# Four sequences through mLSTM, Fourier mix and MLP: a second folded batch, named PSUM banks, and two recurrences started later

## The chip, the cores and the metric

The kernel runs on one core of a Trainium2 chip. The core has a matrix engine (TensorE, "PE" in the profile; its weight loads are listed apart as "PEld"), a vector engine (VectorE, "DVE"), a scalar engine (ScalarE, "ACT"), a general engine (GpSimd, "POOL") and a queue engine (SyncE, "SP") that issues most DMA transfers. Each engine works through its own queue in program order and waits on semaphores for the others. PE writes its results to PSUM, eight banks in this kernel; DVE and ACT read them from there. The metric is the device time of one launch in microseconds (us): the median of several runs. Everything is float32.

## The reference, cut to what matters

Four batches, 8 heads, 768 steps, 40 numbers per head. A gated recurrence gives `y`, the heads are joined to 320 columns, and a Fourier mix followed by a two-layer MLP is applied, with residuals:

```python
for t in range(S):
    m_new = np.maximum(f_gate[:, :, t] + m, i_gate[:, :, t])
    f_stab = np.exp(f_gate[:, :, t] + m - m_new)
    i_stab = np.exp(i_gate[:, :, t] - m_new)
    C = f_stab * C + i_stab * np.einsum('bhd,bhe->bhde', vt, kt)
    n = f_stab * n + i_stab * kt
    y[:, :, t] = sigmoid(o_gate_t) * (C @ qt) / np.maximum(np.abs(n @ qt), 1.0)

X = np.fft.fft(np.fft.fft(x, axis=1), axis=2)        # x: (4, 768, 320)
u = x + np.real(X)
un = (u - mean(u)) / np.sqrt(var(u) + 1e-06)
out = u + np.maximum(un @ w_ch1, 0.0) @ w_ch2        # 320 -> 1280 -> 320
```

(The recurrence is abbreviated: broadcasts are left out.)

## The kernel before

The batches are numbered b = 0 to 3 in the code; "second batch" is b = 1. Each goes through three stages, and different batches are in different stages at the same time.

**Recurrence.** The 768 tokens of a batch are six chunks c = 0 to 5 of 128. A chunk is computed in matrix form on PE: scores of queries with keys, products with the values, and a state that is carried from chunk to chunk (all these small products stand on L547). For b = 1, 2, 3 `plan_halves` spaces the chunks three slots apart. Of a chunk planned at slot s: loads on SP at s − 6 (q and k, L484; k and v, L486), gate tables and masks soon after, the output gate at s − 2; `mlstm_scale_q` (POOL, L528) at s − 2; `mlstm_scale_v` (POOL) and `mlstm_exp` (ACT) at s − 1; scores and state products on PE at s; `halves_decay` (POOL) and `halves_add` (DVE, L703, "C add") at s, s + 1 and s + 2; `halves_weigh` (DVE, L708) at s + 1; `halves_from_state` and `halves_from_chunk` (PE) at s + 3; `mlstm_finish` (DVE, L752 to L759) at s + 4, which reads the heads' PSUM banks and writes the chunk's 128 tokens into x. All chunks share those heads' banks, so `halves_from_state` of a chunk waits for `mlstm_finish` of the chunk before.

**Fourier mix.** The real part of the two-dimensional transform is two sets of products with cosine and sine tables. Tokens t and 768 − t are first folded into sums and differences (`mix_fold`, on DVE, and POOL for small parts), pair p = 2, 1, 0 as their chunks are finished; x_done are the slots of that. For b = 2 and 3 they are folded once more (`mix_fold_again`, L860 the first of its two DVE operations), so that each product covers only every other table column: `mix_products_again` (L903) instead of `mix_products` (L912, L913, L915). `mix_seq` and `mix_tail` issue those products into PSUM tiles pz (two) and pzt, which are copied to SBUF as Z and Zt. `mix_feat` multiplies them with the feature tables into a tile pu for each p (L946). `mix_add` (DVE, L963 to L974) adds pu to the tokens of two chunks, one call for each, and takes the statistics; `mix_center` (ACT, L982) subtracts the mean; `mix_turn` (PE, L989) transposes a token block into a tile put, and `mix_turn_out` (ACT, L994) copies it out.

**MLP.** The first layer in `mlp_in` for b = 0 (L1067, L1058) and in blocks of four steps for b > 0 (L1129, L1134, with DVE's h adds on L1138); the second in `mlp_out` for b = 0 (L1192) and `mlp_out_pair` for b > 0 (L1248), into tiles po; the residual with the row's scale is DVE's L1198, and the store follows it on SP (L1201).

**Order.** A plan written by hand sets it: `at(slot, phase, function, ...)` puts a call into a slot and a phase, and the calls are issued in the order of (slot, phase). The phases are EVAC 0, FILL 1, MAIN 2 and FILL_PE 3, with fractions between. Each engine's queue has that order; a call in a later slot can therefore stand in the way of one that another engine waits for, on any of the five queues. The MLP of b = 0 lies in slots 31 to 62 (its `mlp_out` in 51 to 62), that of b = 1 in 63 to 94 (blocks to 82, pairs from 83), b = 2 in 95 to 126, b = 3 from 127. The mix of b = 1 starts at slot 54, of b = 2 at 83, of b = 3 at 115. The recurrences start at 32, 51 and 83.

**Banks.** Four PSUM banks hold all tiles of the mix and the MLP (pz, pzt, pu, put, pm, po). Each has a pool tag with one buffer, so a new tile in a bank waits until the last reader of the tile before it is done, also when this reader stands in a later slot. `bank(name, shape, n)` takes bank n, or, without n, the next one of a string written out by hand. `MIX` names banks: "z" for pz, "zt" for pzt, "u" for pu in the order p = 0, 1, 2, "ut" for put in the order of `ORDER` (0, 5, 1, 4, 2, 3).

Of the kernel before, what the change touches and what calls it, by code (L numbers as in the profile page):

```python
# [19 lines left out]
L = 128  # L20
# [6 lines left out]
DM = H * D  # L27
# [3 lines left out]
TG = NT // 2  # L31
# [5 lines left out]
NC = HALF_D + 1  # L37
COL = (0, L + 1, 2 * L + 2)
LAST = 2 * L + 1
NK = HALF + 2  # L40
# [7 lines left out]
ORDER = (0, 5, 1, 4, 2, 3)  # L48
# [9 lines left out]
def kernel(  # L58
# [34 lines left out]
    def bank(name, shape, n=None):  # L93

        return ps_m.tile(shape, FP, name=name, tag=f"pm{next(turn) if n is None else n}")
# [34 lines left out]
    def at(slot, phase, fn, *args):  # L130
        plan.setdefault((slot, phase), []).append((fn, args))
# [7 lines left out]
    EVAC, FILL, MAIN, FILL_PE = range(4)  # L139
# [406 lines left out]
    def product(out, w, x, start):  # L546
        nc.tensor.matmul(out, w, x, start=start, stop=True, skip_group_check=True)  # L547
# [234 lines left out]
    def plan_halves(b, s0, stride=3):  # L782
        at(s0 - 2, FILL + 0.7, halves_start, b)
        for c in range(NT):
            s = s0 + stride * c
            end = c == NT - 1
            t = 22 + 2 * c if b == 1 and c < 3 else s - 6
            at(t, FILL, mlstm_load, b, c)
            at(t, FILL, mlstm_load_max, b, c)
            at(t + 1 if c < 2 or b > 1 else s - 5, FILL, mlstm_load_decay, b, c)  # L790
            at(s - 2, FILL, mlstm_load_o, b, c)
            at(s - 2, FILL + 0.1, mlstm_scale_q, b, c)
            at(s - 2, FILL + 0.15, halves_alone, b, c)
            at(s - 1, FILL, mlstm_scale_v, b, c)
            at(s - 1, FILL, mlstm_exp, b, c, 0)
            at(s - 1, FILL + 0.5, mlstm_exp, b, c, NP)
            at(s, FILL, mlstm_mask, b, c)
            at(s, FILL_PE + 2.05, halves_scores, b, c)
            at(s, FILL_PE + 2.5, halves_to_state, b, c)
            for i in range(2):  # L800
                at(s + i, FILL + 0.05, halves_decay, b, c, i)
                at(s + 1 + i, FILL - 0.2, halves_add, b, c, i)
            at(s + 1, FILL, halves_weigh, b, c)
            at(s + 3, MAIN - 0.1 if end else FILL_PE, halves_from_state, b, c)
            at(s + 3, MAIN if end else FILL_PE + 0.5, halves_between, b, c)
            at(s + 3, FILL_PE + 3, halves_from_chunk, b, c)
            at(s + 3, FILL_PE + 0.6, mlstm_tanh, b, c)
            at(s + 4 + int((b, c) in ((2, 2), (3, 1))), FILL + 0.05, mlstm_finish, b, c)

# [4 lines left out]

    mixes = {}

    MIX = {"z": (2, 3), "zt": 2, "u": (3, 2, 2), "ut": (3, 3, 3, 3, 2, 3)}

    def copy(eng, out, in_):
        (nc.scalar.copy if eng == 0 else nc.vector.tensor_copy)(out=out, in_=in_)
# [41 lines left out]
    def mix_seq(b, p, parts):  # L864


        k = mixes.setdefault(b, Mix())
        if p == TG - 1:
            k.pz = getattr(k, "pz", []) + [bank("pz", [L, NK], MIX["z"][i] if b > 1 else None) for i in parts]
        for i in parts:  # L870
            if b < 2:
                mix_products(p, k.pz[i], i, slice(0, L))
            else:
                for product in mix_products_again(k, k.pz[i], i, slice(0, L)):
                    product()

    def mix_tail(b, p):

        k = mixes[b]
        if p == TG - 1:  # L880
            k.pzt = bank("pzt", [L, NK], MIX["zt"] if b > 1 else None)
        halves = [k.pzt[i * 64:(i + 1) * 64] for i in range(2)]
        if b < 2:
            for i in range(2):
                mix_products(p, halves[i], i, slice(L, PAD))
        else:

            a, z = (mix_products_again(k, halves[i], i, slice(L, PAD)) for i in range(2))
            for product in (a[0], z[0], a[1], z[1], a[2], z[2], a[3]):
                product()  # L890
# [17 lines left out]
    def mix_products(p, out, i, m):  # L908
        fm = slice(i * PAD + m.start, i * PAD + m.stop)
        kw = dict(stop=(p == 0), skip_group_check=True)  # L910
        if i == 0 and p == TG - 2:
            nc.tensor.matmul(out[:, 1:NK:2], fe[:, p, fm], ds_sb[:, p, 0, 1:NK:2], start=False, **kw)  # L912
            nc.tensor.matmul(out[:, 0:NK:2], fe_odd[:, m], ds_sb[:, p, 0, 0:NK:2], start=False, **kw)  # L913
        else:
            nc.tensor.matmul(out, fe[:, p, fm], ds_sb[:, p, i], start=(p == TG - 1), **kw)  # L915
# [12 lines left out]
    def mix_feat(b, p):  # L928

        k = mixes[b]
        m = slice(COL[p], COL[p] + L)
        pu = k.pu[p] = bank("pu", [L, DM + 1 + NC], MIX["u"][p] if b > 1 else None)
        if b == 0:
            products = ((pu[:, 0:DM + 1], k.Z[:, 0, m], dd_sb[:, 0]), (pu[:, 0:DM + 1], k.Z[:, 1, m], dd_sb[:, 1]),
                        (pu[:, 0:DM + 1], k.Zt[:, m], dd_sb[:, 2]))
        else:
            products = ((pu[:, 0:NC], k.Z[:, 0, m], dd_sb[:, 0, 0:NC]), (pu[:, NC:DM], k.Z[:, 1, m], dd_sb[:, 1, 1:HALF_D]),  # L940
                        (pu[:, 0:DM], k.Zt[:, m], dd_sb[:, 3, 0:DM]))
        if p == TG - 2:
            last, own = slice(LAST, LAST + 1), pu[0:1, DM + 1:]
            products += ((own, k.Z[:, 0, last], dd_sb[:, 0, 0:NC]), (own, k.Zt[:, last], dd_sb[:, 3, 0:NC]))
        for i, (o, z, t) in enumerate(products):
            nc.tensor.matmul(o, z, t, start=(i == 0), stop=(i in (2, 4)), skip_group_check=True)  # L946
# [37 lines left out]
    def mix_turn(b, c):  # L984

        k = mixes[b]
        pt = k.pt[c] = bank("put", [L, 3, L], MIX["ut"][ORDER.index(c)] if b > 1 else None)
        for ch in range(3):
            nc.tensor.transpose(pt[:, ch, :], k.uc[c].rearrange("p two n -> p (two n)")[:, ch * L:(ch + 1) * L], ident)  # L989

# [27 lines left out]
    def plan_mix(b, s0, x_done, s_feat, s_add, s_turn):  # L1018
        for j in range(TG):
            p = TG - 1 - j  # L1020
            at(x_done[j] + (b > 1 and j == TG - 1), FILL + 0.5 if b < 2 else FILL_PE + 0.2, mix_fold, b, p)
            if b == 0:
                at((s0 - 4, s0 - 2, s0)[j], FILL_PE + 4, mix_seq, b, p, (0, 1))
                at((s0 - 2, s0 - 2, s0)[j], FILL_PE + 4, mix_tail, b, p)
            elif b == 1 or j == 0:
                if b > 1:
                    for step, slot in enumerate((x_done[-1] + 2, x_done[-1] + 6)):
                        at(slot, FILL_PE + 0.25, mix_fold_again, b, step)
                at(s0, FILL_PE + 4, mix_seq, b, p, (0,))
                at(s0 + 1, FILL_PE + 4, mix_seq, b, p, (1,))  # L1030
                at(s0 + 2, FILL_PE + 4, mix_tail, b, p)
        for i in range(2):
            at(s0 + 1 if b == 0 else s0 + 1 + i, FILL, mix_seq_out, b, i)
        at(s0 + (1 if b == 0 else 3), FILL + 0.1, mix_tail_out, b)
        for p in range(TG):
            at(s_feat[p], FILL_PE + 4, mix_feat, b, p)
        for c, a, t in zip(ORDER, s_add, s_turn):
            at(a, FILL if b < 2 else MAIN + 0.5, mix_add, b, c)
            at(t, FILL + 0.1, mix_center, b, c)
            at(t, FILL_PE + (5 if b == 0 or c in ORDER[:4] else -0.1), mix_turn, b, c)  # L1040
            if b > 0:
                at(t, FILL_PE + 6, mix_turn_out, b, c)
            elif t < s_mlp:
                at(t + 1, FILL + 0.2, mix_turn_out, b, c)
            else:
                at(t + 1, EVAC, mix_turn_out, b, c)
# [31 lines left out]
    def hidden(gr, f):  # L1078
        return hid[gr, f % 2][:, f // 2 * TG * L:(f // 2 + 1) * TG * L]
# [107 lines left out]
    def mlp_out(b, gr, i, half):  # L1187
        k = mixes[b]
        if half == 0:
            k.po = bank("po", [L, DM])  # L1190
        for f in range(half * NFF // 2, (half + 1) * NFF // 2):
            nc.tensor.matmul(k.po, hidden(gr, f)[:, i * L:(i + 1) * L], w2_sb[:, f, :], start=(f == 0), stop=(f == NFF - 1))  # L1192

# [83 lines left out]
    MLP_SLOTS = NT // TG * (NFF + 2 * TG)  # L1277
# [69 lines left out]
    s_mlp = 31  # L1347
    plan_batch(0, 0, 22, s_mlp)
    plan_batch(1, 32, 54, s_mlp + MLP_SLOTS)
    plan_batch(2, 51, 83, s_mlp + 2 * MLP_SLOTS)  # L1350
    plan_batch(3, 83, 115, s_mlp + 3 * MLP_SLOTS)
    for n in range(4):
        at(s_mlp + 2 * NFF + 1 + n, FILL + 0.4, weight_sums, n)
        at((56, 57, 58, 75)[n], FILL + 0.4, out_weight_sums, n)
# [162 lines left out]
```

## Time and profile before

| | us |
|---|---|
| runs of the kernel | 402.89, 404.14, 404.44 (median 404.14) |
| the profiled execution | 404.67, its span 402.9 |
| PE busy | 387.8 |
| DVE busy | 279.8 |
| ACT busy | 178.5 |
| POOL busy | 128.0 |

The profile shows one execution. A line of a group or of the timeline gives start and duration, engine, line of the code, operation, output and inputs, and in square brackets how long the engine was idle ahead of it and what ended that. The line of PE's waits gives the total, how often, and the longest. Over the span the mean granted clock of PE is 0.991. The DMA engines are most busy in the first 110 us; the mean over the span is 109 GB/s.

### The profile page before, as it was taken

To read this page: it belongs to the slowest core of one execution; us is meant where nothing else is said; L and a number is where in the kernel's file an instruction comes from. 1 tells how busy PE (TensorE), PEld (TensorE's weight loads), DVE (VectorE), ACT (ScalarE), POOL (GpSimd) and SP (SyncE) were. 2 spreads that over 40 slices of the span, in tenths; PEclk is the share of its full clock that TensorE was granted. 3 is DMA by queue.
4 is the path that set the end of the run, shared out by engine and by line. 5 is a ranking of instruction groups with operands and counts; after the bars stand their busy time and mean duration, and the time that the engine had idled before them with its cause. 6 is when DMAs were issued, how large, how long until landed. Compare 5 with 4: busy or idle time off the path is not lost.

```text
span 402.9 us, 10837 instructions
## 1 busy us (share of the span) xinstructions
PE 387.8 (96%) x4324; PEld 283.3 (70%) x4324; DVE 279.8 (69%) x668; ACT 178.5 (44%) x513; POOL 128.0 (32%) x231
## 2 busy tenths in 40 slices
PE   8999999999969999999999998999999999999996
PEld 6887555556546776856569887855579997556996
DVE  7789976898867519787665689777663795336652
ACT  6898867576530213553562214544440023454000
POOL 5744425466945412261145304351200000020000
PEclk9999999989989999999999999999999999999999
DMA  7979499677752424365100525300000000000000
GB/s 197 278 227 320 121 240 257 194 242 240 191 151 70 142 87 131 109 196 150 54 26 2 157 82 170 103 20 2 1 0 18 17 34 33 2 0 0 34 34 34
DMA packets 22766, 43.96 MB, mean 109 GB/s; under 512 B 3492, under 2 KB 11388, under 8 KB 22588
## 3 DMA queue, kind: packets, MB, share of 16 engines
q1 hardware_dynamic: 22716, 43.27, 36.0%
q8 instruction: 34, 0.56, 0.5%
q14 instruction: 16, 0.13, 0.1%
HBM read 39.16 MB, written 4.10 MB: 107 GB/s over the span
## 4 chain that ended last, share of the span: by engine, by line
PE 80%; DVE 13%; issue 2%; POOL 2%; ACT 2%; DMA 0%; DVEq 0%; SPq 0%; POOLq 0%; ACTq 0%
PE po L1248 20%; PE pm L1129 16%; PE po L1192 8%; PE pm L1134 6%; PE ph L547 5%; PE ps L547 4%; PE pu L946 4%; PE pm L1067 4%; PE put L989 2%; PE pz L903 1%; PE pz L915 1%; DVE so L756 1%; PE pM L230 1%; PE pm L1058 1%; DVE x L759 1%
## 5 line engine op out<-in xcount | busy, mean ns | idle before, releaser
L1138 DVE TENSOR_TENSOR h<-h,pm 128x384 f32<-128x384 f32 x60 | 30.7, 550 | 30.6 <-PE pm L1129 16.5
L1198 DVE SCALAR_TENSOR_TENSOR x<-po,rstd,x 128x160 f32<-128x160 f32 (+1 forms) x69 | 27.0, 394 | 35.0 <-PE po L1248 32.3
L1129 PE MATMUL pm<-uT,w_sb 128*128 128x384 f32 x90 | 37.8, 507 | 0.2 <-DVE uT L1117 0.2
L543 POOL TENSOR_SCALAR_AFFINE_SELECT W<-W 64x512 f32<-64x512 f32 x36 | 27.9, 775 | 31.5 <-ACT W L518 30.4
L696 POOL TENSOR_TENSOR C<-C,decB 128x164 f32<-128x164 f32 x33 | 17.4, 528 | 62.1 <-DVE C L703 58.4
L518 ACT ACTIVATE W<-W,colT 128x64 f32<-128x64 f32 x144 | 36.5, 338 | 0.0
L1192 PE MATMUL po<-w_sb,h 128*128 128x320 f32 x120 | 35.2, 444 | 0.0
L1013 POOL TENSOR_TENSOR t<-rstd 128x6 f32<-128x6 f32 x12 | 2.6, 216 | 90.1 <-DVE v L1007 89.7
L1248 PE MATMUL po<-T,S 128*128 128x160 f32 x180 | 28.1, 303 | 2.6 <-DVE x L1198 2.6
L528 POOL TENSOR_TENSOR qg<-qk,Gb 128x512 f32<-128x512 f32 x21 | 27.3, 1298 | 9.5 <-DMA Gb<-G_d 9.5
L1192 PEld LDWEIGHTS po<-w_sb,h 128*128 128x128 f32 x120 | 22.7, 194 | 10.0 <-issue 1.5
L1067 PE MATMUL pm<-uT,w_sb 128*128 128x384 f32 x80 | 29.5, 505 | 0.1
L1248 PEld LDWEIGHTS po<-T,S 128*128 128x128 f32 x180 | 25.3, 190 | 4.5 <-DVE x L1198 3.4
L1248 PE MATMUL po<-w_sb,h 128*128 128x160 f32 x180 | 26.3, 300 | 0.0
L1248 PEld LDWEIGHTS po<-w_sb,h 128*128 128x128 f32 x180 | 25.2, 190 | 1.5 <-DVE x L1198 0.3
L994 ACT COPY uT<-put 128x384 f32<-128x384 f32 x24 | 11.1, 478 | 32.7 <-PE put L989 32.6
L1134 PE MATMUL pm<-uT,w1t_sb 64*128 64x384 f32 x120 | 25.2, 510 | 0.2 <-DVE h L1138 0.2
L1129 PEld LDWEIGHTS pm<-uT,w_sb 128*128 128x128 f32 x90 | 15.4, 189 | 14.0 <-DVE h L1138 4.9
L1185 ACT ACTIVATE h<-h 128x384 f32<-128x384 f32 x45 | 23.1, 520 | 2.0 <-DVE h L1138 2.0
L982 ACT ACTIVATE uc<-x 128x384 f32<-128x384 f32 x24 | 14.5, 614 | 18.9 <-DVE x L974 18.9
L703 DVE TENSOR_TENSOR C<-C,ps 128x164 f32<-128x164 f32 x33 | 10.5, 317 | 16.2 <-PE ps L547 13.6
L1067 PEld LDWEIGHTS pm<-uT,w_sb 128*128 128x128 f32 x80 | 14.5, 194 | 9.7 <-issue 1.4
(240 smaller groups left out, 860.8 us busy)
## 6 DMA issues: line engine op xcount, KB each, us to landing
kvt<-in_kv SPq DMA_DIRECT2D x24, 336.0 KB
qk<-in_qkT SPq DMA_DIRECT2D x48, 160.0 KB
raw<-in_w SPq DMA_DIRECT2D x10, 640.0 KB
Gb<-G_d SPq DMA_DIRECT2D x42, 128.0 KB
W<-M_d SPq DMA_DIRECT2D x36, 128.0 KB
so<-in_o SPq DMA_DIRECT2D x24, 160.0 KB
out<-x SPq DMA_DIRECT2D x24, 160.0 KB
ds_sb<-in_dft_s SPq DMA_DIRECT2D x1, 1158.0 KB
```

Of the source, the lines that this page charges most:

```text
L518: nc.scalar.activation(out=k.W[:, h, :], in_=M, func=AF.Exp, scale=-1.0, bias=colT[:, c, 0, b * H + h:b * H + h + 1])
L528: nc.gpsimd.tensor_tensor(out=k.qg[:, :, t], in0=k.qk[:, 0, :, t], in1=k.Gb[:, :, t], op=OP.mult)
L543: nc.gpsimd.affine_select(out=W, in_=W, compare_op=OP.is_ge, fill=0.0, base=base, pattern=[[0, H], [-1 if back else 1, LH]], channel_multi ...
L547: nc.tensor.matmul(out, w, x, start=start, stop=True, skip_group_check=True)
L1067: nc.tensor.matmul(k.pm[i], w1_sb[:, ch, f0:f0 + L], u[2 * ch], start=(ch == 0 and not ahead), stop=(ch == 1 and ahead), skip_group_check= ...
L1129: nc.tensor.matmul(bank, w, u, start=start, stop=True, skip_group_check=True)
L1134: nc.tensor.matmul(bank, block(w1t_sb, i)[rows], mlp_u(gr, 1)[rows], start=False, stop=True, skip_group_check=True)
L1138: nc.vector.tensor_tensor(out=h, in0=h, in1=bank, op=OP.add)
L1185: nc.scalar.activation(out=h, in_=h, func=AF.Relu, scale=-1.0)
L1192: nc.tensor.matmul(k.po, hidden(gr, f)[:, i * L:(i + 1) * L], w2_sb[:, f, :], start=(f == 0), stop=(f == NFF - 1))
L1198: nc.vector.scalar_tensor_tensor(out=u, in0=po, scalar=k.rstd[:, c:c + 1], in1=u, op0=OP.mult, op1=OP.add)
L1248: nc.tensor.matmul(po, a[:, f], w[:, f], start=start and f == 0, stop=f == half - 1, skip_group_check=True)
```

## The change

Four things are changed.

- The second batch (b = 1) is folded twice as well: both steps of `mix_fold_again` run in the slot of its last fold, and its sequence products are the half-column ones. For b = 2 and 3 the steps move to two and four slots behind the last fold, from two and six.
- The banks of that batch's mix are named: pz and pzt as for the later batches, pu by a new list "u1" and put by a new list "ut1". The po tiles of b = 0 alternate between banks 0 and 1. The string of banks stays as it is.
- The recurrences of b = 2 and 3 start at slots 54 and 86.
- Their `mlstm_finish` is planned at s + 4 in phase MAIN + 0.4, behind the residual or h add of that slot, where it was FILL + 0.05; the two chunks that had one slot more lose it.

```diff
-            at(s + 4 + int((b, c) in ((2, 2), (3, 1))), FILL + 0.05, mlstm_finish, b, c)
+            at(s + 4, FILL + 0.05 if b == 1 else MAIN + 0.4, mlstm_finish, b, c)
...
-    MIX = {"z": (2, 3), "zt": 2, "u": (3, 2, 2), "ut": (3, 3, 3, 3, 2, 3)}
+    MIX = {"z": (2, 3), "zt": 2, "u": (3, 2, 2), "ut": (3, 3, 3, 3, 2, 3), "u1": (3, 2, 3), "ut1": (2, 3, 2, 3, 2, 3)}
...
-            k.pz = getattr(k, "pz", []) + [bank("pz", [L, NK], MIX["z"][i] if b > 1 else None) for i in parts]
+            k.pz = getattr(k, "pz", []) + [bank("pz", [L, NK], MIX["z"][i] if b > 0 else None) for i in parts]
         for i in parts:
-            if b < 2:
+            if b == 0:
                 mix_products(p, k.pz[i], i, slice(0, L))
...
-            k.pzt = bank("pzt", [L, NK], MIX["zt"] if b > 1 else None)
+            k.pzt = bank("pzt", [L, NK], MIX["zt"] if b > 0 else None)
...
-        if b < 2:
+        if b == 0:
             for i in range(2):
                 mix_products(p, halves[i], i, slice(L, PAD))
...
-        pu = k.pu[p] = bank("pu", [L, DM + 1 + NC], MIX["u"][p] if b > 1 else None)
+        pu = k.pu[p] = bank("pu", [L, DM + 1 + NC], MIX["u" if b > 1 else "u1"][p] if b > 0 else None)
...
-        pt = k.pt[c] = bank("put", [L, 3, L], MIX["ut"][ORDER.index(c)] if b > 1 else None)
+        pt = k.pt[c] = bank("put", [L, 3, L], MIX["ut" if b > 1 else "ut1"][ORDER.index(c)] if b > 0 else None)
...
-            elif b == 1 or j == 0:
-                if b > 1:
-                    for step, slot in enumerate((x_done[-1] + 2, x_done[-1] + 6)):
-                        at(slot, FILL_PE + 0.25, mix_fold_again, b, step)
+            elif j == 0:
+                for step in range(2):
+                    at(*((x_done[-1], FILL + 0.55) if b == 1 else (x_done[-1] + 2 + 2 * step, FILL_PE + 0.25)),
+                       mix_fold_again, b, step)
...
-            k.po = bank("po", [L, DM])
+            k.po = bank("po", [L, DM], (gr * TG + i) % 2)
...
-    plan_batch(2, 51, 83, s_mlp + 2 * MLP_SLOTS)
-    plan_batch(3, 83, 115, s_mlp + 3 * MLP_SLOTS)
+    plan_batch(2, 54, 83, s_mlp + 2 * MLP_SLOTS)
+    plan_batch(3, 86, 115, s_mlp + 3 * MLP_SLOTS)
```

## The prediction

> **What bounds the kernel now.** I read the page's busy times first, then the chain that ended last, then the waits of TensorE (PE), then the timelines of PE and VectorE (DVE) around the edits.
>
> ```profile
> PE 387.8 (96%) x4324; PEld 283.3 (70%) x4324; DVE 279.8 (69%) x668; ACT 178.5 (44%) x513; POOL 128.0 (32%) x231
> ...
> PE 80%; DVE 13%; issue 2%; POOL 2%; ACT 2%; DMA 0%; DVEq 0%; SPq 0%; POOLq 0%; ACTq 0%
> ...
> PE ph L547 <- DVE x L759: 3.1, 1, 3.1
> PE po L1248 <- DVE x L1198: 2.6, 2, 1.9
> ```
>
> PE is busy 387.8 of 402.9 us and in order: a product taken off it is worth its own time, and any wait at its head is lost at full price. The two wait lines are the largest holes near the edits: 3.1 us for the heads' banks (about 111 us, plan slot 49), and 0.75 and 1.85 us (236 and 248 us) for residuals of the second batch's output stage. The busy share of DVE (69%) hides where it is late: the new waits below all hang on its order.
>
> **The clock, as rows.** Windows of time: us from:to, then PE, PEld, DVE, ACT, POOL busy, granted PE clock, DMA share, GB/s.
>
> ```profile
> 82.00:85.30 3.30, 3.30 (x87) 2.92 (x82) 3.20 (x8) 1.52 (x6) 1.44 (x3) 0.50 0.72 207
> ...
> 111.00:114.00 3.00, 0.00 (x0) 0.00 (x0) 2.79 (x8) 0.47 (x2) 0.00 (x0) 1.00 0.65 181
> ...
> 116.00:119.50 3.50, 3.50 (x40) 2.18 (x37) 1.40 (x5) 2.75 (x10) 3.19 (x9) 0.51 0.22 72
> ...
> 250.00:254.00 4.00, 4.00 (x109) 3.83 (x113) 3.29 (x13) 0.48 (x2) 0.06 (x1) 1.00 0.14 49
> ```
>
> PE stood 1.0 us at 80.5 and 3.08 us at 110.98; soon after each the clock was 0.50 for 3.4 us, which loses 1.7 us. After the 1.85 us at 248.0 and the 0.75 at 235.6 it stayed 1.00. So a stop of about 3 us costs itself and, by these rows, possibly 1.7 more.
>
> **Part 1, the fold of the second batch (b = 1).** Its sequence products leave L912–915 for the half-column ones of L903. Time on PE now: first tile 132.70 to 134.88, 2.17; second 1.95; tail 2.14; together 6.26. The same products of the third batch, already folded: 1.56 + 1.34 + 1.52 = 4.42 (at 213.7, 217.8, 222.0). PE has no idle there, so the difference counts: −1.84. DVE gets two 128x384 operations of about 0.55 (row L860) in slot 52, behind the last fold (ends 128.2). The first product that needs them starts at 132.6 now and could come at about 130.7 when the third batch's first heads leave slots 51 to 53; DVE would end at 129.3, so about 1.4 us of cover remains: cost 0. If the cover is gone, at most those 1.1 us.
>
> **Part 2, the named banks.** A tile in a bank waits for the last reader of the tile before it. For b = 1 the list for pu becomes (3, 2, 3) and for put (2, 3, 2, 3, 2, 3). So the first put (block 0, slot 59) takes the bank of pu p=1, whose last reader is mix_add(1, 4), planned in slot 60; before, it waited for mix_add(1, 5) of slot 58. The second put (block 5, slot 60) takes the bank of pu p=2, which PE has only just filled, and waits for mix_add(1, 3) of slot 61; before, it waited for mix_add(1, 4). These are PE's rows now, then DVE's:
>
> ```profile
> 150.16 0.70 PE L946 MATMUL pu<-dd_sb,Zt 128*128 128x320 f32 x2
> ...
> 158.00 0.49 PE L989 MATMUL put<-ident,uc 128*128 128x128 f32 x3
> 158.33 2.86 PE L1192 MATMUL po<-w_sb,h 128*128 128x320 f32 x10
> ...
> 163.65 0.70 PE L946 MATMUL pu<-dd_sb,Zt 128*128 128x320 f32 x2
> ```
>
> ```profile
> 150.90 0.33 DVE L968 TENSOR_TENSOR x<-x,pu 128x161 f32<-128x161 f32 x1 [1.33 <-PE pu L946]
> ...
> 161.06 0.31 DVE L971 TENSOR_TENSOR x<-x,pu 128x159 f32<-128x159 f32 x1
> ...
> 164.39 0.33 DVE L968 TENSOR_TENSOR x<-x,pu 128x161 f32<-128x161 f32 x1 [1.33 <-PE pu L946]
> ...
> 166.73 0.32 DVE L971 TENSOR_TENSOR x<-x,pu 128x159 f32<-128x159 f32 x1
> ```
>
> From pu p=0 on (150.9) DVE runs without a gap: two mix_adds, the weighing, weight sums, a finish, a residual, a C add, mix_add(1, 1), and mix_add(1, 4), whose last reader ends at 161.37. The change only reorders some of these. PE is at its put at 158.17: 161.37 − 158.17 = 3.2 us. Behind the put on PE stand the output products of slot 60, the heads and pu p=2: all of them move. DVE then waits for PE, so it starts pu p=2 fresh: 164.39 to 167.04 for both mix_adds up to L971, and PE stands from 164.3: 2.7 us. Behind it stand the third put and slot 61. Neither has a cover, as PE takes nothing out of order: +5.9 (each wait could be some 0.3 shorter or longer).
>
> Clock: 3.2 and 2.7 are nearest to the 3.08 row, which was followed by 3.4 us at half speed. I take 1.7 for each, +3.4; the low end is 0 (the 1.85 row). [...] The rows disagree: 1.0 us was enough at 80.5, and 1.85 was not at 248.
>
> The rest of the new lists stays hidden: po of the first batch alternates two banks and waits for a residual a whole product group (2.7 us) old; pzt waits for a copy one slot back; pu p=0 waits for the copy of pz that it reads anyway.
>
> **Part 3, recurrences of b = 2 and 3 three slots later.** Everything of a chunk moves: loads of q, k, v, gates and masks on SP (they keep their six slots of lead), scaling, masks and decays on POOL, exponentials on ACT, joins on DVE, heads on PE. PE's heads only change place. Three places where it shows:
> - Slot 49, the 3.08 us stop. PE waits for finish(1, 4), the end of a DVE stretch without gaps from 101.8. In it L456 takes 1.77 us (1.15 at 99.32) and L452 1.08 beside POOL's qg of the third batch (109.01 to 110.85), which leaves. L456 back to 0.83 (as at 78.72) and L452 to 0.82: −1.2; I take −1.0, a stop of about 2. Whether the slow clock at 116 goes too is open: bounds 0 to −2.9. I keep the clock loss, as 1.0 us sufficed at 80.5.
> - Slots 87 and 88. Finish(3, 0) waits 1.87 us on DVE for a store and holds a residual and two mix_adds; PE stands 0.75 at 235.6. That finish goes to slot 90: −0.7. In slots 90 and 91 DVE has as much ahead of the residual as before (finish(3, 0) where finish(3, 1) was), so the 1.85 us stays. Bounds 0 to −2.6.
> - Slots 69 to 72 and 101 to 104: one more chunk beside the MLP blocks. DVE has about 3.3 us of it per chunk; idle before the blocks' own h adds (L1138 waits 16.5 us for PE) covers it. The heads wait for the finish of the same slot distance as before. I take 0, with +0.5 as upper bound.
>
> **Part 4, finish behind residual and h add.** In slot 64, finish (1.7 to 2.1 us) holds the h add that frees a bank: the next eight products of L1134 take 2.43 instead of 1.49 us (177.58). The like at 266.0 loses 0.3 to 0.9. After it the h add goes first. Behind finish wait C adds and the next h add, at 178.55 now as then, so not all of it is kept: −0.9; bounds 0 to −1.8.
>
> **The sum**, from the profiled execution, 404.67 us (span 402.9, and 1.8 around it; 0.53 above the median of 404.14): −1.84 + 3.2 + 2.7 + 3.4 − 1.0 − 0.7 − 0.9 = +4.86, so 409.5 against 404.67, or **409.0** against the median.
>
> **Rivals.**
> - The clock holds through one new stop, or through both, as after 248: 407.3, or 405.6. For: two of the four stops above left it alone. Against: the 3.08, the nearest in length, did not.
> - Faster: the puts do not stop PE, 409.0 − 5.9 − 3.4 = 399.7. It decides when DVE ends mix_add(1, 4) by 158.2, 3.2 us sooner. For: the weighing, sums and finish ahead of it (0.66 + 0.98 + 1.7) are work that PE does not need there, and the change moves that finish. Against: its new place is still slot 58.
> - The stop of slot 49 goes whole, with its slow clock: −4.8 in place of −1.0, so 405.2. It needs finish(1, 4) 3 us earlier; the contended rows hold only 1.2 of that, unless L450 (1.30) and the folds at 106 shrink too.
> - The change doesn't do what it says: the folded products wait for DVE or for a bank, and the 1.84 is not gained: 410.8. Against: 1.4 us of cover.
>
> **How the numbers follow.** Forecast 0.42; one slow clock 0.17; no slow clock 0.14; slot 49 whole 0.08; puts without a stop 0.10; fold without gain 0.09. A measurement of this kernel can tell about 0.5%, so 402.1 to 406.2 is "same": 0.14 + 0.08 = 0.22 there, 0.68 above, 0.10 below. All gains of parts 3 and 4 at their ends and no slow clock: 404.14 − 1.84 + 5.9 − 2.9 − 2.6 − 1.8 = 400.9; none of them, both slow clocks and the +0.5: 404.14 − 1.84 + 5.9 + 3.4 + 0.5 = 412.1. The range, 402.5 to 411.0, leaves out the fast case and most of the tail above. The forecast's own: 407.8 to 410.5.
>
> **What would show it.** New lines in PE's waits: put L989 behind DVE x L971, twice, 3.2 and 2.7 us; half clock for some 3.4 us behind each. No L912 to L915 for b = 1, and 4.4 us on its products in place of 6.26. The wait of ph for x L759 at about 2 us instead of 3.1; po for x L1198 once at 1.9. The eight L1134 products of slot 65 at about 1.5 to 2.0. I am wrong if PE's puts do not wait (DVE earlier than I read, or another last reader), or if the later recurrences empty a stage that I took as covered.

## The result

The changed kernel takes 410.84 us (median; 410.13 to 411.84) against 404.29 us for the kernel before: ratio 1.0158, interval 1.0122 to 1.0195. The forecast was 409.0, with a range of 402.5 to 411.0. The profiled execution took 411.20 us, its span is 409.5.

Page and chain of the changed kernel, busy time and shares of the span:

```profile
PE 388.7 (95%) x4324; PEld 283.9 (69%) x4324; DVE 279.3 (68%) x670; ACT 178.6 (44%) x513; POOL 130.5 (32%) x231
...
PE 65%; DVE 20%; DMA 5%; issue 4%; POOL 3%; ACT 2%; SPq 0%; DVEq 0%; POOLq 0%; ACTq 0%
```

PE is busy 388.7 us, 0.9 more than before, while the span grew by 6.6: the change added idle time. DVE's share of the chain went from 13% to 20%. PE's waits in the changed kernel (us in total, times, longest):

```profile
PE put L989 <- DVE x L971: 6.2, 2, 3.3
PE ph L547 <- DVE x L759: 2.3, 1, 2.3
...
PE po L1248 <- DVE x L1198: 1.1, 1, 1.1
...
PE pm L1129 <- ACT uT L994: 0.9, 1, 0.9
```

The first line is the forecast's, and new. The second shrank from 3.1, the third from 2.6 in two waits. The last is new, and the forecast did not have it. On PE's timeline (start, duration, instruction, idle time ahead of it and what ended that) it looks like this:

```profile
146.89 2.96 PE L1192 MATMUL po<-w_sb,h 128*128 128x320 f32 x10
153.20 0.87 PE L989 MATMUL put<-ident,uc 128*128 128x128 f32 x3 [3.35 <-DVE x L971]
153.86 5.33 PE L1192 MATMUL po<-w_sb,h 128*128 128x320 f32 x10
...
162.12 0.70 PE L946 MATMUL pu<-dd_sb,Zt 128*128 128x320 f32 x2
165.65 1.50 PE L989 MATMUL put<-ident,uc 128*128 128x128 f32 x6 [2.83 <-DVE x L971]
166.94 3.93 PE L1192 MATMUL po<-w_sb,h 128*128 128x320 f32 x10
```

The ten products of po, 2.86 us before, take 5.33 and 3.93 us behind the stops. Windows of the same stretch (us from:to, busy PE, PEld, DVE, ACT, POOL, granted PE clock, DMA share, GB/s) say why:

```profile
153.20:159.00 5.80, 5.80 (x13) 3.70 (x13) 0.56 (x2) 1.50 (x3) 0.00 (x0) 0.51 0.09 31
159.00:162.80 3.80, 3.80 (x151) 3.13 (x150) 0.88 (x2) 0.52 (x2) 1.20 (x2) 1.00 0.02 6
...
165.65:169.20 3.55, 3.55 (x11) 2.77 (x12) 2.80 (x9) 1.47 (x3) 0.00 (x0) 0.52 0.30 96
```

The granted clock (the value behind POOL's) averages 0.51 over 5.8 us behind the first stop, which loses 2.8 us, and 0.52 over 3.55 us behind the second, which loses 1.7.

**A measure for the experiments.** The clock falls in some executions of a kernel and not in others. Four executions of e_sums below had spans of 395.4, 398.0, 397.4 and 395.4 us at mean granted clocks of 1.000, 0.991, 0.996 and 1.000; span times clock is 394.4 to 395.8. That product is called "time at full clock" here, and the rest of the span "clock loss". It is an approximation (idle time counts in the mean clock too), but it separates what a kernel does from how often the clock fell. Means over the executions that were compared (without six slow ones of the kernel before, over 1.5% longer than its fastest):

| kernel | executions | at full clock, us | clock loss, us |
|---|---|---|---|
| before | 46 | 398.9 | 3.9 |
| changed | 4 | 403.7 | 5.5 |
| e_fold | 10 | 397.3 | 4.9 |
| e_late | 5 | 397.2 | 2.8 |
| e_shift | 10 | 398.2 | 2.5 |
| e_put0 | 10 | 399.9 | 3.7 |
| e_banks | 10 | 396.5 | 1.7 |
| e_sums | 4 | 395.3 | 1.3 |
| e_exp | 10 | 397.3 | 2.8 |
| e_both | 4 | 396.8 | 1.2 |
| e_finish | 4 | 395.1 | 1.3 |
| e_join | 4 | 393.5 | 0.4 |

Within a kernel the time at full clock scatters by 0.3 to 1.0 us (standard deviation). The experiments were run in three groups, each with executions of the kernel before, whose means are 399.0 (with e_fold, e_banks, e_put0, e_shift), 398.6 (e_sums, e_exp, e_finish, e_both) and 399.1 (e_late, e_join); a difference between kernels of two groups is good to some 0.5 us. The change costs 403.68 − 398.94 = 4.74 at full clock and 5.52 − 3.87 = 1.65 in clock loss: 6.4 of span.

### The profile page after: what moved, and what is told of

Same layout as the page of the kernel before. It is cut to its first block, busy times and chain, and to the rows that moved or that the text cites. A ratio compares the mean times of both kernels' runs of the same rounds, so it can differ in the third digit from the quotient of the medians.

```text
span 409.5 us, 10830 instructions
## 1 busy us (share of the span) xinstructions
PE 388.7 (95%) x4324; PEld 283.9 (69%) x4324; DVE 279.3 (68%) x670; ACT 178.6 (44%) x513; POOL 130.5 (32%) x231
## 4 chain that ended last, share of the span: by engine, by line
PE 65%; DVE 20%; DMA 5%; issue 4%; POOL 3%; ACT 2%; SPq 0%; DVEq 0%; POOLq 0%; ACTq 0%
PE po L1248 20%; PE pm L1129 13%; PE po L1192 7%; PE pm L1134 5%; PE pu L946 3%; PE ph L547 2%; DVE so L756 2%; DMA W<-M_d 2%; PE pz L903 2%; DMA raw<-in_w 2%; PE ps L547 2%; PE put L989 1%; DVE h L1138 1%; PE pM L230 1%; DVE x L759 1%
## 5 line engine op out<-in xcount | busy, mean ns | idle before, releaser
L1198 DVE SCALAR_TENSOR_TENSOR x<-po,rstd,x 128x160 f32<-128x160 f32 (+1 forms) x69 | 27.2, 394 | 50.5 <-PE po L1248 36.9
L1138 DVE TENSOR_TENSOR h<-h,pm 128x384 f32<-128x384 f32 x60 | 30.6, 550 | 28.1 <-PE pm L1129 12.6
L1129 PE MATMUL pm<-uT,w_sb 128*128 128x384 f32 x90 | 37.8, 507 | 1.1 <-ACT uT L994 0.9
L1192 PE MATMUL po<-w_sb,h 128*128 128x320 f32 x120 | 37.6, 469 | 0.0
L1192 PEld LDWEIGHTS po<-w_sb,h 128*128 128x128 f32 x120 | 24.4, 208 | 10.6 <-issue 2.9
L1134 PE MATMUL pm<-uT,w1t_sb 64*128 64x384 f32 x120 | 26.3, 511 | 0.4 <-DVE h L1138 0.4
L1248 PEld LDWEIGHTS po<-w_sb,h 128*128 128x128 f32 x180 | 25.2, 190 | 1.5 <-DVE x L1198 0.3
L1129 PEld LDWEIGHTS pm<-uT,w_sb 128*128 128x128 f32 x90 | 15.5, 189 | 14.8 <-DVE h L1138 5.9
L1134 PEld LDWEIGHTS pm<-uT,w1t_sb 64*128 64x128 f32 x120 | 12.8, 185 | 12.9 <-issue 8.2
```

What stands on the lines that cost most here:

```text
L1129: nc.tensor.matmul(bank, w, u, start=start, stop=True, skip_group_check=True)
L1134: nc.tensor.matmul(bank, block(w1t_sb, i)[rows], mlp_u(gr, 1)[rows], start=False, stop=True, skip_group_check=True)
L1138: nc.vector.tensor_tensor(out=h, in0=h, in1=bank, op=OP.add)
L1198: nc.vector.scalar_tensor_tensor(out=u, in0=po, scalar=k.rstd[:, c:c + 1], in1=u, op0=OP.mult, op1=OP.add)
L1248: nc.tensor.matmul(po, a[:, f], w[:, f], start=start and f == 0, stop=f == half - 1, skip_group_check=True)
```

## The experiments

**Other banks: e_banks and e_put0.** The theory is that PE's stops come from the bank lists alone. The first run names banks whose readers are done; the second mends only the first put.

```diff
 e_banks
-"u1": (3, 2, 3), "ut1": (2, 3, 2, 3, 2, 3)
+"u1": (3, 2, 2), "ut1": (3, 3, 0, 3, 2, 0)
 e_put0
-"u1": (3, 2, 3), "ut1": (2, 3, 2, 3, 2, 3)
+"u1": (3, 2, 3), "ut1": (3, 3, 2, 3, 2, 3)
```

> The changed kernel with other banks for pu and put of b = 1: u1 (3, 2, 2), ut1 (3, 3, 0, 3, 2, 0); nothing else differs. Theory: the stops of 3.35 and 2.83 us at L989 and the 0.88 us at the first pm tile go, and with them the half clock behind them (about 3.0 and 1.7 us): 410.8 - 11.8 = 399.0, ratio to before 0.987. Rival (the later recurrences are what costs, the stops only move the idle time): 404 to 408, with other waits of PE in the place of those. Rival (stops cost only themselves, the half clock comes anyway): 403.8.

> The changed kernel with ut1 (3, 3, 2, 3, 2, 3): only the first put gets a bank whose readers are done; the second put still waits for mix_add(1, 3), the first pm tile still for the copy of the last put. Theory: 410.8 - 3.35 - 3.0 (first stop and the half clock behind it) = 404.5; one wait of 2.8 us at L989 left, with about 3.4 us of half clock behind it. Rival (one stop of 2.8 us alone is too short for the clock, two in 15 us were needed): 402.8 and full clock throughout.

e_banks: 399.95 us, ratio 0.9904 (0.9865 to 0.9944). e_put0: 405.47 us, ratio 1.0033 (1.0002 to 1.0065). At full clock e_banks is 403.7 − 396.5 = 7.2 us below the changed kernel; the three stops in the profile were 3.35 + 2.83 + 0.88 = 7.06. The clock loss fell by 3.8, where 4.7 was expected. PE's timeline of e_banks over the same instructions:

```profile
150.30 2.96 PE L1192 MATMUL po<-w_sb,h 128*128 128x320 f32 x10
153.09 0.49 PE L989 MATMUL put<-ident,uc 128*128 128x128 f32 x3
153.42 2.86 PE L1192 MATMUL po<-w_sb,h 128*128 128x320 f32 x10
...
159.74 0.82 PE L989 MATMUL put<-ident,uc 128*128 128x128 f32 x6
160.39 2.86 PE L1192 MATMUL po<-w_sb,h 128*128 128x320 f32 x10
```

No idle time ahead of a put, and po at 2.86 us. The 0.88 us went with the lists too: in the changed kernel the last put (block 3) has bank 3, and the first pm tile of the next slot takes bank 3 from the string and has to wait for ACT's copy of that put. In e_banks that put has bank 0. So the first rival (idle time only moves) falls. The second (the half clock comes anyway) falls for this stretch: the granted clock of e_banks is 1.00 in every window of 3 us from 120 to 180 us.

e_put0 kept one stop of 2.84 us (it ends at 161.11) and the 0.88, and the granted clock was 0.77 in the window from 159 to 162 us and 0.66 from 162 to 165: 3.4 us at half clock. So one such stop was enough here, and the rival with two falls.

**The fold alone: e_fold.** On the kernel before:

```diff
-            elif b == 1 or j == 0:
-                if b > 1:
-                    for step, slot in enumerate((x_done[-1] + 2, x_done[-1] + 6)):
-                        at(slot, FILL_PE + 0.25, mix_fold_again, b, step)
+            elif j == 0:
+                for step in range(2):
+                    at(*((x_done[-1], FILL + 0.55) if b == 1 else (x_done[-1] + 2 + 4 * step, FILL_PE + 0.25)),
+                       mix_fold_again, b, step)
...
-            if b < 2:
+            if b == 0:
...
-        if b < 2:
+        if b == 0:
```

> The kernel before with the second fold of b = 1 alone (banks from the string, recurrences and finishes as before). Theory (the named banks carry the loss, the fold is worth its products): 4.42 us on the sequence products of b = 1 in place of 6.26, no new wait of PE ahead of pz, so 404.3 - 1.8 = 402.5, ratio 0.9955. Rival (the folded products wait for DVE, or the gain is lost to a later wait): 404 to 405.

Measured 403.74 us, ratio 0.9985 (0.9945 to 1.0025): by time alone it can't be told from no change. At full clock it is 397.25 against 398.94, −1.7, close to the 1.8 worked out; PE's waits hold no new line for pz of b = 1. The gain was in part covered by a clock loss of 4.9 us, 1.0 more than the mean of before. Why it was larger in these ten is open; in the profiled one the page has the clock at 0.8 in the slice from 240.4 to 250.4 us, in the output stage of b = 1 (longest stop 1.8 us), where the kernel before kept full clock (1.00 from 228 to 258 us).

**Recurrences and finish: e_shift and e_late.** On the kernel before, the later recurrences with the moved finish, and then without it:

```diff
 both
-    plan_batch(2, 51, 83, s_mlp + 2 * MLP_SLOTS)
-    plan_batch(3, 83, 115, s_mlp + 3 * MLP_SLOTS)
+    plan_batch(2, 54, 83, s_mlp + 2 * MLP_SLOTS)
+    plan_batch(3, 86, 115, s_mlp + 3 * MLP_SLOTS)
...
-                    for step, slot in enumerate((x_done[-1] + 2, x_done[-1] + 6)):
+                    for step, slot in enumerate((x_done[-1] + 2, x_done[-1] + 4)):
 e_shift
-            at(s + 4 + int((b, c) in ((2, 2), (3, 1))), FILL + 0.05, mlstm_finish, b, c)
+            at(s + 4, FILL + 0.05 if b == 1 else MAIN + 0.4, mlstm_finish, b, c)
 e_late
-            at(s + 4 + int((b, c) in ((2, 2), (3, 1))), FILL + 0.05, mlstm_finish, b, c)
+            at(s + 4, FILL + 0.05, mlstm_finish, b, c)
```

> The kernel before with parts 3 and 4 alone: recurrences of b = 2 and 3 at slots 54 and 86, their finishes behind the residual or h add, fold steps two and four slots behind the last fold; no second fold of b = 1, no new named banks. Theory: the stop of slot 49 is 2.3 in place of 3.1 us (-0.8), the output stage of b = 1 loses 1.1 in place of 2.6 us (-1.1 with the 0.4 lost at L1248 by issue), the L1134 products of slots 77 and 109 lose 1.3 and 0.4: sum about -0.2 to -0.5, so 403.9, or 402.2 if the clock also stays up behind slot 49. Rival (this is the part that costs): 407 to 409.

> The kernel before with the later recurrences alone (slots 54 and 86, fold steps two and four slots behind the last fold); finishes in FILL + 0.05 at s + 4, no second fold of b = 1, no named banks. Theory (the runs so far: the move of the finish costs 1.4 us, the later recurrences gain 2.1): span times granted clock 398.9 - 2.1 = 396.8, some 399.5 us. Rival (finish and recurrences help only together): 398.2 or more, as with both.

e_shift: 401.66 us, ratio 0.9961 (0.9916 to 1.0006); 398.2 at full clock. e_late: 401.86 us, ratio 0.9931 (0.9893 to 0.9969); 397.2 at full clock. So neither is what costs. The later recurrences gain 1.8 at full clock, and the move of the finish takes 1.0 of it back (2.0 and 1.1 when each run is compared with the kernel before in its own group). The next run shows the same on the other base.

**The finish undone: e_finish.** On e_banks:

```diff
-            at(s + 4, FILL + 0.05 if b == 1 else MAIN + 0.4, mlstm_finish, b, c)
+            at(s + 4, FILL + 0.05, mlstm_finish, b, c)
```

> The kernel of e_banks with part 4 undone: mlstm_finish of b = 2 and 3 in FILL + 0.05 again, ahead of the residual or h add of its slot. Theory (the move of the finish is worth little in the blocks, 0.1 at slot 65, and up to 0.8 in the output stage, where the 1.85 us became 1.08): 0.5 to 1.5 us more than e_banks, 400.5 to 401.5; a wait of 0.5 to 1.9 us of po for x L1198 comes back. Rival (the forecast's 0.9 in the blocks was right): L1134 of slots 65 and 97 0.9 longer than in e_banks.

A miss, in sign: 397.73 us, ratio 0.9834 (0.9775 to 0.9892), and 395.1 at full clock, 1.4 *less* than e_banks (1.1 by the groups' own executions of before). The groups of eight L1134 products, one for each block, show where. First e_banks, then e_finish, blocks of b = 1:

```profile
173.13 2.35 PE L1134 MATMUL pm<-uT,w1t_sb 64*128 64x384 f32 x8
...
198.95 0.91 PE L1134 MATMUL pm<-uT,w1t_sb 64*128 64x384 f32 x2
200.25 1.55 PE L1134 MATMUL pm<-uT,w1t_sb 64*128 64x384 f32 x6 [0.39 <-DVE h L1138]
```

```profile
169.03 2.42 PE L1134 MATMUL pm<-uT,w1t_sb 64*128 64x384 f32 x8
...
194.92 1.56 PE L1134 MATMUL pm<-uT,w1t_sb 64*128 64x384 f32 x8
```

Slot 65 (first rows) is the same in both: the finish did not hold it, or something else holds it at once. In slot 97 the late finish does gain: 2.34 us there against 2.64. Slot 77 takes 2.85 us (0.91 and 1.55, with 0.39 idle) where the finish is late and 1.56 where it is early. DVE's timeline of the changed kernel ahead of slot 77:

```profile
202.26 1.48 DVE L1138 TENSOR_TENSOR h<-h,pm 128x384 f32<-128x384 f32 x3 [2.43 <-PE pm L1134]
203.66 0.16 DVE L752 TENSOR_SCALAR den<-ph 128x8 f32<-128x8 f32 x1
...
205.23 0.98 DVE L1220 TENSOR_TENSOR w_sb<-w_sb 128x800 f32<-128x800 f32 x1
...
206.69 0.48 DVE L833 TENSOR_TENSOR eo<-x 128x320 f32<-128x320 f32 x1
...
208.27 0.55 DVE L1138 TENSOR_TENSOR h<-h,pm 128x384 f32<-128x384 f32 x1
```

DVE idles 2.43 us ahead of the h adds of slot 73. A finish in FILL + 0.05 lies in that gap and costs nothing. Behind the h adds, it starts a queue: finish, weight sums, the scale (L1002 to L1007), the last fold of b = 2, and only then the h add of slot 76, which PE waits for. The waits for the output stage hardly differ (po for x L1198: 1.1 in e_banks, 1.3 in e_finish and in e_late, 2.6 before), so that gain belongs to the later recurrences, not to the finish.

**Two holds in the blocks: e_sums, e_exp, e_both.** On e_banks: the last weight sums into the gap of slot 72, the exponentials of ACT behind the copy of their slot, and both.

```diff
 e_sums
-        at((56, 57, 58, 75)[n], FILL + 0.4, out_weight_sums, n)
+        at((56, 57, 58, 72)[n], FILL + 0.4 if n < 3 else MAIN + 0.4, out_weight_sums, n)
 e_exp
-            at(s - 1, FILL, mlstm_exp, b, c, 0)
-            at(s - 1, FILL + 0.5, mlstm_exp, b, c, NP)
+            at(s - 1, FILL if b == 1 else MAIN + 0.4, mlstm_exp, b, c, 0)
+            at(s - 1, FILL + 0.5 if b == 1 else MAIN + 0.4, mlstm_exp, b, c, NP)
```

> The kernel of e_banks with out_weight_sums(3) in slot 72 behind the h add, in place of slot 75. Theory (the 1.3 us that the L1134 products of slot 77 lose are DVE's: finish, 0.98 of weight sums, and the last fold of b = 2, 1.65, stand ahead of the h add of slot 76): those products go from 2.85 to about 1.9 us; 0.9 us less than e_banks, 399.0. Rival (the fold alone, or ACT's copy, holds them): still 2.5 or more, 400.0.

> The kernel of e_banks with the exponentials of b = 2 and 3 (eight of ACT's L518, 2.0 us) behind the MLP block's ACT copy of their slot (phase MAIN + 0.4) in place of ahead of it. Theory (with the finish out of the way it is the ACT copy of L1170 behind those exponentials that holds the second four L1134 products of slots 65 and 97): 2.34 and 2.35 go to about 1.6 us, 1.5 us less than e_banks, 398.5. Rival (DVE's h add still holds them): both stay at 2.3, 400.0. Costs that could show: the masks of POOL and the weighing come later; the stop of slot 49 is b = 1's and stays.

> The kernel of e_banks with the edits of e_sums and e_exp together. If the two holds are separate, 2.4 us less than e_banks: 397.6, ratio to before 0.984. If one only uncovers the other: 398.5 to 399.0.

e_sums: 398.1 us, ratio 0.9837 (0.9779 to 0.9896); slot 77 went from 2.85 to 1.95 us, as expected. This confirms DVE's queue as the hold there: taking out the 0.98 us of weight sums gave back 0.90.

e_exp: 401.08 us, ratio 0.9927 (0.9888 to 0.9967), and at full clock 0.7 more than e_banks, where 1.5 less was expected. The hold of slot 65 was found, and nothing was gained:

```profile
170.82 1.56 PE L1134 MATMUL pm<-uT,w1t_sb 64*128 64x384 f32 x8
179.61 2.30 PE L1134 MATMUL pm<-uT,w1t_sb 64*128 64x384 f32 x8
```

Slot 65 went from 2.35 to 1.56, so ACT's copy behind eight exponentials was what held it in e_banks. But the eight of slot 69 then took 2.30 (1.58 in e_banks), and pm L1129 waited for h L1138 twice, 1.2 us in all. e_both, 399.99 us, ratio 0.9874 (0.9809 to 0.9938), shows the same rows: one hold uncovers another. It is 1.5 us slower at full clock than e_sums, and above both values expected.

**The stop of slot 49: e_join.** On e_finish; the last weight piece's join (L450 to L456) stands on DVE ahead of finish(1, 4), which PE waits for. It goes one slot later:

```diff
-            at(s, FILL + phase, fn)
+            at(s + int(s == 47), FILL + phase, fn)
```

> The kernel of e_finish with the join of the last weight piece (L450 to L456 on DVE, 3.2 us) in slot 48, behind finish(1, 4), in place of slot 47. Theory (the stop of slot 49 is DVE's queue ahead of finish(1, 4), 3.2 us of it this join): the wait of ph for x L759 goes from 2.3 us to under 0.3, and with it the half clock that sometimes follows; 2 to 3.5 us less than e_finish, 394.5 to 395.5, ratio 0.976. Rival (finish(1, 4) then waits for something else, or the join arrives late for po of slot 52): 397 to 398.

395.23 us, ratio 0.9796 (0.9757 to 0.9834): the fastest kernel here, 2% below before. PE's waits:

```profile
PE po L1248 <- DVE x L1198: 1.3, 1, 1.3
PE ps L547 <- DVE C L703: 1.0, 1, 1.0
...
PE ph L547 <- DVE x L759: 0.4, 1, 0.4
```

The wait for x L759 went from 2.3 to 0.4 us; at full clock it is 1.6 us faster than e_finish, and the clock loss fell to 0.4.

## Why the prediction was right, point by point

The sign, the place and most of the size were right: 409.0 forecast, 410.84 measured. That it came so near is in part luck, as errors cancelled: the clock was put 1.7 too high, the wait at the first pm tile (0.9) was left out, and the finish was wrong in sign, by some 2 us. The terms, in us, by the runs:

| term of the sum | forecast | measured |
|---|---|---|
| fold of b = 1 | −1.84 | −1.7 (e_fold) |
| stops at the two puts | +5.9 | +6.2 (3.35 and 2.83) |
| stop at the first pm tile | none | +0.9 |
| clock | +3.4 | +1.7 net |
| stop of slot 49 | −1.0 | −0.8 (3.08 to 2.30) |
| output stage of b = 1 | −0.7 | −1.5 (2.6 to 1.1), less 0.5 of issue |
| extra chunk in the blocks | 0 | 0 |
| finish moved | −0.9 | +1.0 to +1.4 |

The parts measured singly add up: at full clock, fold −1.7, later recurrences −1.8, finish +1.0, banks +7.2, together +4.7, and 4.7 was measured. So the named banks of pz, pzt and po, which no run tried alone, cost nothing that shows.

- **Banks.** The working held: the waits come from the last reader, and DVE's order gives their length within 0.15 us. One sentence failed: "The rest of the new lists stays hidden". It followed the lists through pz, pzt, pu and po, and not on to the next tile that takes a bank from the string. That is where 0.88 us were.
- **Clock.** Half clock came at both puts, and the term was mis-sized, in both directions. Behind the two puts 2.8 + 1.7 were lost in the profile, not 3.4. But the forecast let every other loss stand ("I keep the clock loss, as 1.0 us sufficed at 80.5"), and the profile had none at slot 49 nor at 81 (1.00 in every window from 75 to 150 us): net +1.7.
- **Length of a stop.** In the profiles of this case half clock came with the stops of 3.35 and 2.83 us (changed kernel), 3.25 (e_fold), 3.08 (before) and 2.84 (e_put0), and in part with much shorter ones (below). The nearest row, 3.08, decided rightly for both puts.
- **Part 4** failed. The step was "the next eight products of L1134 take 2.43 instead of 1.49 us ... After it the h add goes first", −0.9. The h add did go first, and the group still took 2.34: ACT's copy (L1170), which stands behind eight exponentials, held the second half (e_exp). And "Behind finish wait C adds and the next h add" left out slots 73 to 76, where weight sums and a fold stand in the same queue: +1.3 there and 0.4 in slot 109.
- **Output stage.** The 0.75 us went as said. The 1.85 was to stay and became 1.08; the two sums (L1234) ahead of that residual took 1.65 and 1.35 us before and 0.83 and 0.81 after, more than the 0.77 gained. That they are the cause is read from the rows and not shown by a run, and what slowed them before was not tried; e_late has 1.3 there without the moved finish, so it belongs to the later recurrences.
- **Extra chunk.** In e_late every L1134 group of the blocks is as before (2.42 in slot 65, 1.56 to 1.59 in the others up to slot 81): it costs nothing while the finish is early.

## What to carry to other kernels

When tiles share named buffers, write down for each bank the last reader of every tile and its place in that reader's queue, and follow the list until the first tile that is named by something else; here three waits came from one line of numbers, worth 7.2 us, while the same change with other numbers is 1% faster than the kernel before. Moving work behind the instruction that someone waits for helps only if nothing else is waited for right behind it: look for the gap in which the work lay free. Before a hold is removed, find the second-latest thing that the waiting instruction needs.

## What the runs showed of the hardware

**Stops and the clock.** One profile of each of the twelve kernels was read: the stops in PE's timelines and waits, the granted clock in windows of 3 us from 75 to 180 us. For the output stage the clock is that of windows of 1 us (before) and of the page (e_fold). In us:

| stop of PE | with half clock | at full clock (1.00) |
|---|---|---|
| slot 49 and puts, 2.8 to 3.4 | before 3.08, e_fold 3.25, changed 3.35 and 2.83, e_put0 2.84 | none |
| slot 49, 2.1 to 2.3 | e_banks 2.15, e_shift 2.29, e_exp 2.29 | changed 2.30, e_put0 2.13, e_late 2.14, e_sums 2.29, e_finish 2.29, e_both 2.14 |
| output stage of b = 1, 1.8 to 1.9 | e_fold 1.8 | before 1.85 |
| near 81 us, 0.9 to 1.0 | before 1.00, e_banks 1.01, e_put0 1.01, e_late 1.00, e_both 0.97 | changed 0.92, e_fold 0.92, e_shift 1.01, e_sums 1.00, e_exp 1.00, e_finish 1.00, e_join 1.01 |

All five stops of 2.8 us and more came with half clock. Of the shorter ones the length does not tell: 2.29 us had it in e_shift and e_exp and not in e_sums and e_finish. What else decided it was not shown by a run.

**When and how long.** In the kernel before the clock was at 0.50 from 81.9 to 85.3 us and from 116.0 to 119.4, 3.4 us each; the stops ahead of these ended at 81.55 and 114.06. In the changed kernel it was at 0.50 for 6.8 us from 152.0 on, 1.2 us before the first stop ended (153.20), and for 3.4 us from 165.7 on, where the second ended at 165.65.

**What it costs.** The 3.4 us at 0.50 lose 1.7, and how often that came differs between executions: the 46 of the kernel before had mean granted clocks from 0.982 to 1.000, and most of their scatter goes with it (standard deviation 1.6 us in span, 0.8 at full clock). (The four of the changed kernel had 0.986 or 0.987; theirs, 1.7 us from end to end, has another cause, which is open.) A gain of 1.7 us, as that of e_fold, can be hidden behind it.
